# A gated mix of linear attention and an MLP block: wk by column halves, a second x chunk turned on PE, LN1 and w4 moved around the M stage

## The chip, the cores and the metric

The kernel runs on one core of one Trainium2 chip. The metric is the time of one execution on the device, in microseconds (us), as the median of several runs. The engines are TensorE (PE; its weight loads are shown as PEld), VectorE (DVE), ScalarE (ACT), GpSimd (POOL) and SyncE (SP). SP, ACT and POOL also issue DMA transfers.

## What is computed

One input x of 2048 rows and 640 columns goes through two blocks, whose results are mixed row by row with a gate:

```python
g = sigmoid((x * gate_w).sum(-1, keepdims=True))
qkv = x @ wqkv                                   # 32 heads of 20
pq, pk = phi(q), phi(k)                          # phi(t) = (t + 1 if t > 0 else exp(t)) + 1e-6
kv = einsum("bhsd,bhse->bhde", pk, v);  z = pk.sum(over s)
a = (pq @ kv) / (pq @ z + 1e-6)  @ wo            # linear attention
h = gelu(layernorm(x) @ w1)                      # B block
hs = (the four column groups of h, shifted by +1, -1, +2, -2 rows) @ w2
x1 = x + hs
b = x1 + gelu(layernorm(x1) @ w3) @ w4           # w3: 640 x 1728, w4: 1728 x 640
out = g * a + (1 - g) * b
```

Everything is bfloat16 in memory, with float32 sums.

## The kernel before

Rows are cut into 16 chunks (tiles) of 128, and into four tiles of 512 for the second half. Columns of 640 are five blocks of 128 (`DC`), or two halves of 320 (`HD`), the most that the code puts into one PSUM bank. All PSUM tiles are pairs of banks from one pool of four (`pair()`). The order of the instructions on every engine is the order in which the code writes them; the framework adds the waits. DMA queues are in order too: SP carries nearly all transfers.

The stages, in PE's order:

- **Start and K** (lines 126 to 225). x chunk 0 (line 126), gate_w and the five row blocks of wk, 128 x 640 each (`load_wk`, lines 128 to 132), are issued in turn on SP and ACT. Then SP issues seven DMA transposes (`load_xT`, line 133) that bring x chunks 1 to 15 in turned form into `xT`, then wq, x itself, wv, w1, wo, w2 and w3. Chunk 0 alone is turned on PE (lines 206 to 215): five transposes into two PSUM tiles (`turns`), each copied to `xT` by DVE; gate_w is turned in between and copied into column 640 of `wk_sb`, so that the K matmuls also give the gate's logit. `warmup` (line 200) issues filler matmuls on a constant: before the first work, and one of 256 columns between the row blocks of chunk 0. `k_mm` (line 186) does one chunk: for each of the five row blocks a left (320) and a right (321) matmul. `k_evac` copies the logit out and applies phi (`phi`, lines 177 to 184: one ACT and two DVE instructions).
- **Q** (`q_unit`, line 228), ten units of 1024 rows.
- **G** (`g_unit`, line 302): pk-transposed times x, with the statistics of the first layer norm (LN1) between the units, and `ln1_apply` (line 292), which normalises a chunk on DVE and turns it by a DMA transpose on SP into `lnxT[t]`. Three tiles of 512 rows are applied here.
- **w1 of tiles 0 and 1, kv, denominators** (`w1_unit`, line 336; `kv_unit`; `den_mm` and `den_evac`, lines 243 to 254, with a long DVE reciprocal). After w1 of tile 1 come LN1's last tile (lines 391 and 392), the release of the first stage's buffers, and the load of w4 on POOL's queue (lines 396 to 398).
- **M** (`m_unit`, line 373): kv times wo, five units of 16 small matmuls, each evacuated by ACT (line 381); then `r_unit`.
- **w2 of tile 0 with the second layer norm (LN2)** (`w2_unit`, line 408; `ln2_apply`, line 428, again with DMA transposes on SP), then w1 of tiles 2 and 3.
- **The loop over four tiles** (line 548): w3 with gelu (`w3_unit`), w2 of the next tile, attention's product with M (`att_unit`), then w4 (`w4_tile`) and the stores.

The kernel's own lines that the change touches:

Of the kernel before, what the change touches and what calls it, by code (L numbers as in the profile page):

```python
# [9 lines left out]
BF16 = mybir.dt.bfloat16  # L10
# [6 lines left out]
def kernel(  # L17
# [13 lines left out]
    nc = tc.nc  # L31
    P = 128
    S, D = A_x.shape[1], A_x.shape[2]
    F = B_w3.shape[1]
    H, Dh = 32, 20
    NCH = S // P
    TS = 512
    NT = S // TS
    CPT = TS // P
    DC = D // P  # L40
    HD = D // 2
    FF = F // P
    FR = F - FF * P
# [13 lines left out]
    wqkv_v = A_wqkv.rearrange("(c p) f -> p c f", p=P)  # L57
# [11 lines left out]
    def pair():  # L69
        return ps.tile([P, 2, 512], F32, name="pp")  # L70


    x_sb = const.tile([P, NCH, D + 2], BF16)
# [12 lines left out]
    ident = const.tile([P, P], BF16)  # L86
    g5 = const.tile([DC, P], BF16)
# [19 lines left out]
    wk_sb = st1.tile([P, DC, D + 16], BF16)  # L107
    gT = wk_sb
    xT = st1.tile([P, DC, S], BF16)
# [5 lines left out]
    sp, aq, gq = nc.sync, nc.scalar, nc.gpsimd  # L115

    def load_x(c0, c1):
        sp.dma_start(x_sb[:, c0:c1, 0:D], x2[c0 * P:c1 * P, :].rearrange("(c p) d -> p c d", p=P))

    def load_xT(c0, c1):  # L120
        sp.dma_start_transpose(xT[:, :, c0 * P:c1 * P], x2[c0 * P:c1 * P, :])

    def load_wk(q, dc):
        q.dma_start(wk_sb[:, dc, 0:D], A_wqkv[dc * P:(dc + 1) * P, D:2 * D])

    load_x(0, 1)
    aq.dma_start(g5[:], gate_w.rearrange("(c p) -> c p", p=P))
    load_wk(sp, 1)
    load_wk(aq, 0)
    load_wk(aq, 2)  # L130
    load_wk(sp, 3)
    load_wk(aq, 4)
    for c0, c1 in ((1, 2), (2, 3), (3, 4), (4, 6), (6, 8), (8, 12), (12, 16)):
        load_xT(c0, c1)
    sp.dma_start(wq_sb, wqkv_v[:, :, 0:D])
    load_x(1, 8)
    load_x(8, 12)
    load_x(12, 16)
    sp.dma_start(wv_sb[:], wqkv_v[:, :, 2 * D:3 * D])
# [37 lines left out]
    def phi(dst, src, n):  # L177
        e = e_p.tile([P, 1024], BF16, name="e")
        ev = e[:, 0:n]
        if len(src.shape) == 3:  # L180
            ev = ev.rearrange("p (h e) -> p h e", h=src.shape[1])
        nc.scalar.activation(ev, src, ACT.Exp)  # L182
        nc.vector.tensor_scalar(e[:, 0:n], e[:, 0:n], 1.0, 1e-6, op0=ALU.min, op1=ALU.add)  # L183
        nc.vector.scalar_tensor_tensor(dst, src, 0.0, ev, op0=ALU.max, op1=ALU.add)

    def k_mm(pt, c, dcs, hfs=(0, 1), last=DC - 1):
        for dc in dcs:
            for hf in hfs:
                n = HD + hf
                nc.tensor.matmul(pt[:, hf, 0:n], lhsT=xT[:, dc, c * P:(c + 1) * P],  # L190
                                 rhs=wk_sb[:, dc, hf * HD:hf * HD + n], start=(dc == 0), stop=(dc == last))

    def k_evac(pt, c):
        nc.scalar.copy(ylog[:, c:c + 1], pt[:, 1, HD:HD + 1])
        phi(pk[:, c, :].rearrange("p (h e) -> p h e", h=2), pt[:, :, 0:HD], D)
# [4 lines left out]
    def warmup(n, w=TS):  # L200
        for i in range(n):
            nc.tensor.matmul(warm[:, 1, 0:w], lhsT=one[:, 0:P], rhs=one[:, 0:w], start=True, stop=True)

    warmup(6)
    warmup(3, P)
    kp = pair()
    turns = [(pair()[:, 0, :].bitcast(BF16), a, b) for a, b in ((0, 2), (2, DC))]
    tg = warm[:, 0, :].bitcast(BF16)
    for n, (ptb, a, b) in enumerate(turns):
        for dc in range(a, b):  # L210
            nc.tensor.transpose(ptb[:, (dc - a) * P:(dc - a + 1) * P], x_sb[:, 0, dc * P:(dc + 1) * P], ident[:])
        nc.vector.tensor_copy(xT[:, a:b, 0:P], ptb[:, 0:(b - a) * P].rearrange("p (c s) -> p c s", c=b - a))
        if n == 0:
            nc.tensor.transpose(tg[:, 0:DC], g5[:], ident[0:DC, 0:DC])
            nc.vector.tensor_copy(wk_sb[:, :, D], tg[:, 0:DC])
    warmup(3, P)
    for dc in range(DC):
        k_mm(kp, 0, (dc,))
        if dc < DC - 1:
            warmup(1, 2 * P)  # L220
    k_evac(kp, 0)
    for c in range(1, NCH):
        pt = pair()
        k_mm(pt, c, range(DC))
        k_evac(pt, c)
# [17 lines left out]
    def den_mm():  # L243
        pt = pair()
        for j in range(DC):
            for t in range(NT):
                nc.tensor.matmul(pt[32 * t:32 * (t + 1), 0, :], lhsT=zbd[:, j, :], rhs=pqT[:, j, t * TS:(t + 1) * TS],  # L247
                                 start=(j == 0), stop=(j == DC - 1))
        return pt

    def den_evac(pt):
        nc.scalar.activation(pt[:, 1, :], pt[:, 0, :], ACT.Copy, bias=1e-6)
        with nc.allow_low_precision(reason="rounded after a float32 division, as a copy would"):
            nc.vector.reciprocal(r_bf[:], pt[:, 1, :])
# [9 lines left out]
    def scale_t(t):  # L264
        sl = pqT[:, :, t * TS:(t + 1) * TS]
        nc.vector.tensor_tensor(sl, sl, rb[:, t:t + 1, :].broadcast_to([P, DC, TS]), op=ALU.mult)
# [25 lines left out]
    def ln1_apply(c):  # L292
        t, cc = divmod(c, CPT)
        if cc == 0:
            lnxT[t] = lnx_p.tile([P, DC, TS], BF16, name="lnxT")
        lnx = work.tile([P, D], BF16, name="ln")
        nc.vector.tensor_scalar(lnx[:], x_sb[:, c, 0:D], mv1[:, c, 0:1], rstd1[:, c:c + 1],
                                op0=ALU.subtract, op1=ALU.mult)
        nc.sync.dma_start_transpose(lnxT[t][:, :, cc * P:(cc + 1) * P], lnx[:])
# [55 lines left out]
    def kv_unit():  # L355
        pt = pair()
        for g in range(NG):
            n = heads[g] * Dh
            for fc in range(DC):
                nc.tensor.matmul(pt[:, g // 3, (g % 3) * GW:(g % 3) * GW + n], lhsT=wv_sb[:, fc, row0[g]:row0[g] + P],  # L360
                                 rhs=gT[:, fc, 0:D].rearrange("p (j h i) -> p j h i", j=DC, h=H)
                                 [:, :, head0[g]:head0[g] + heads[g], :], start=(fc == 0), stop=(fc == DC - 1))
        for b, (q, g) in enumerate(pairs_qg):
            h0, h1 = max(8 * q, head0[g]), min(8 * q + 8, head0[g] + heads[g])
            a0, a1 = h0 - head0[g], h1 - head0[g]
            m = bmask5 if g == 5 else bmask
            base = (g % 3) * GW
            nc.vector.tensor_tensor(
                kvT[:, b, :, 4 * (h0 - 8 * q):4 * (h1 - 8 * q)],
                pt[:, g // 3, base:base + heads[g] * Dh].rearrange("p (j a) -> p j a", j=DC)[:, :, 4 * a0:4 * a1],  # L370
                m[:, 4 * a0:4 * a1].unsqueeze(1).broadcast_to([P, DC, 4 * (a1 - a0)]), op=ALU.mult)
# [14 lines left out]
        w1_unit(0, fcs)  # L386
    kv_unit()
    den_evac(den_mm())
    for fcs in w1_split:
        w1_unit(1, fcs)  # L390
    for cc in range(CPT):
        ln1_apply(3 * CPT + cc)
    s1.close()
    w4p = ctx.enter_context(tc.tile_pool(name="w4p", bufs=1))
    w4_sb = w4p.tile([P, FF + 1, D], BF16)
    nc.gpsimd.dma_start(w4_sb[:, 0:FF, :], B_w4[0:FF * P, :].rearrange("(c p) f -> p c f", p=P))
    nc.gpsimd.dma_start(w4_sb[0:FR, FF, :], B_w4[FF * P:F, :])
    nc.gpsimd.dma_start(w4_sb[FR:P, FF, :], B_w4[FF * P:F, :])
    h2p = ctx.enter_context(tc.tile_pool(name="h2p", bufs=1))
    x1p = ctx.enter_context(tc.tile_pool(name="x1p", bufs=8))  # L400
    st = {}
# [26 lines left out]
    def ln2_apply(t, cc):  # L428
        if cc == 0:
            st[t]["lnT"] = lnx_p.tile([P, DC, TS], BF16, name="lnxT")  # L430
        ln = work.tile([P, D], BF16, name="ln")
        nc.vector.tensor_scalar(ln[:], st[t]["x1"][cc][:], st[t]["mv"][:, cc, 0:1], st[t]["rstd"][:, cc:cc + 1],
                                op0=ALU.subtract, op1=ALU.mult)
        nc.sync.dma_start_transpose(st[t]["lnT"][:, :, cc * P:(cc + 1) * P], ln[:])
# [100 lines left out]
    for fcs in w1_split:  # L535
        w1_unit(2, fcs)
        if fcs[0] == 0:
            ln2_apply(0, CPT - 1)
    scale_t(0)
    scale_t(1)  # L540
    for fcs in w1_split:
# [48 lines left out]
```

## Time and profile before

| | us |
|---|---|
| median of 4 runs | 267.38 |
| lowest, highest | 267.05, 267.63 |
| the profiled execution | 267.53 |
| its span, first to last instruction | 265.0 |
| DVE busy | 139.6 |
| ACT busy | 84.2 |
| POOL busy | 22.8 |
| K stage, from PE's first matmul of it to its last | 5.59 to 27.99 |
| M stage, from its first matmul to the first of w2 | 85.2 to 88.5 |

The granted TensorE clock is full from 4.18 us on, and the mean over the span is 1.000. The DMA queues moved 23.62 MB; the share of busy time of the 16 DMA engines is highest in the first 45 us, where all weights and x come in, and it is near full there. After that only the layer norms' transposes, w4 and the stores are left.

A line of the chain of waits is: start, length, engine and what it did; the line number is that of the kernel. A line of the timeline adds the operation, the output and the inputs, the shape, and in brackets the idle time of the engine before it with what ended it.

### The profile page before, as it was taken

To read this page: it belongs to the slowest core of one execution; us is meant where nothing else is said; L and a number is where in the kernel's file an instruction comes from. 1 tells how busy PE (TensorE), PEld (TensorE's weight loads), DVE (VectorE), ACT (ScalarE), POOL (GpSimd) and SP (SyncE) were. 2 spreads that over 40 slices of the span, in tenths; PEclk is the share of its full clock that TensorE was granted. 3 is DMA by queue.
4 is the path that set the end of the run, shared out by engine and by line. 5 is a ranking of instruction groups with operands and counts; after the bars stand their busy time and mean duration, and the time that the engine had idled before them with its cause. 6 is when DMAs were issued, how large, how long until landed. Compare 5 with 4: busy or idle time off the path is not lost.

```text
span 265.0 us, 4251 instructions
## 1 busy us (share of the span) xinstructions
PE 259.1 (98%) x1728; PEld 162.1 (61%) x1744; DVE 139.6 (53%) x270; ACT 84.2 (32%) x122; POOL 22.8 (9%) x58
## 2 busy tenths in 40 slices
PE   7999999999999999999999999999999999999994
PEld 4777555788754654555567556567555566455663
DVE  1688778899946797955412364503464413122132
ACT  1455454321165735622420313330222340333100
POOL 7100010012223040001000001000001000000000
PEclk9999999999999999999999999999999999999999
DMA  7999978016668942000132000042000042000011
GB/s 173 199 194 370 375 238 326 0 28 123 124 116 249 200 87 52 0 0 2 25 74 77 25 0 2 9 90 77 25 0 2 1 99 76 25 0 2 0 49 49
DMA packets 44749, 23.62 MB, mean 89 GB/s; under 512 B 35450, under 2 KB 43642, under 8 KB 44730
## 3 DMA queue, kind: packets, MB, share of 16 engines
q1 hardware_dynamic: 43792, 20.57, 30.8%
q0 software_dynamic: 496, 2.29, 2.7%
q10 hardware_dynamic: 442, 0.49, 0.5%
q8 instruction: 13, 0.21, 0.4%
q14 instruction: 6, 0.05, 0.1%
HBM read 12.21 MB, written 2.62 MB: 56 GB/s over the span
## 4 chain that ended last, share of the span: by engine, by line
PE 95%; DMA 2%; ACT 1%; issue 0%; ACTq 0%; DVE 0%
PE pp L479 22%; PE pp L462 21%; PE pp L307 8%; PE pp L190 8%; PE pp L415 8%; PE pp L446 8%; PE pp L341 8%; PE pp L232 8%; DMA wk_sb<-in_A_wqkv_dram 2%; PE pp L467 1%; PE pp L488 1%; ACT m_sb L381 1%; PE pp L360 1%; PE pp L247 0%; PE pp L379 0%
## 5 line engine op out<-in xcount | busy, mean ns | idle before, releaser
L470 ACT ACTIVATE h<-pp 128x1024 bf16<-128x1024 f32 (+1 forms) x28 | 27.8, 992 | 102.8 <-PE pp L462 94.4
L462 PE MATMUL pp<-lnxT,w_sb 128*128 128x512 bf16 x249 | 59.8, 379 | 0.6
L479 PE MATMUL pp<-w_sb,h 128*128 128x320 bf16 x416 | 57.9, 299 | 0.0
L479 PEld LDWEIGHTS <-h 128*128 128x128 bf16 x416 | 40.0, 98 | 17.0 <-issue 1.9
L462 PEld LDWEIGHTS <-w_sb 128*128 128x128 bf16 x260 | 25.4, 98 | 26.7
L495 DVE SCALAR_TENSOR_TENSOR oc<-pp,omg,x 128x640 bf16<-128x640 f32 x15 | 12.9, 881 | 44.0 <-PE pp L488 27.1
L449 DVE SCALAR_TENSOR_TENSOR x<-pp,gate,x 128x640 f32<-128x640 f32 x16 | 13.9, 868 | 29.4 <-PE pp L446 29.4
L182 ACT ACTIVATE e<-pp 128x640 bf16<-128x640 f32 (+1 forms) x26 | 21.5, 826 | 9.6 <-PE pp L232 9.6
L446 PE MATMUL pp<-m_sb,pqT 128*128 128x320 bf16 x160 | 24.3, 299 | 0.0
L418 DVE TENSOR_TENSOR x<-pp,x_sb 128x640 f32<-128x640 f32 x16 | 13.1, 819 | 21.0 <-PE pp L415 21.0
L415 PE MATMUL pp<-w_sb,hsT 128*128 128x320 bf16 x160 | 23.9, 299 | 0.1
L190 PE MATMUL pp<-wk_sb,xT 128*128 128x320 bf16 (+1 forms) x160 | 22.4, 299 | 0.7 <-DMA wk_sb<-in_A_wqkv_dram 0.7
L307 PE MATMUL pp<-x_sb,pk 128*128 128x320 bf16 (+1 forms) x160 | 22.3, 300 | 0.0
L232 PE MATMUL pp<-xT,hsT 128*128 128x512 bf16 x98 | 21.6, 379 | 0.1
L307 PEld LDWEIGHTS <-pk 128*128 128x128 bf16 x160 | 18.8, 117 | 3.5
L415 PEld LDWEIGHTS <-hsT 128*128 128x128 bf16 x160 | 15.7, 98 | 8.2 <-issue 0.2
L446 PEld LDWEIGHTS <-pqT 128*128 128x128 bf16 x160 | 15.7, 98 | 7.7
L190 PEld LDWEIGHTS <-xT 128*128 128x128 bf16 x160 | 15.6, 98 | 6.8 <-issue 0.8
L341 PE MATMUL pp<-lnxT,w_sb 128*128 128x512 bf16 x77 | 17.8, 379 | 0.2
L232 PEld LDWEIGHTS <-hsT 128*128 128x128 bf16 x100 | 11.8, 118 | 9.7
L277 POOL TENSOR_SCALAR rstd<-mv 128x4 f32<-128x4 f32 (+1 forms) x11 | 3.4, 313 | 148.3 <-DVE mv L283 148.3
L183 DVE TENSOR_SCALAR e<-e 128x640 bf16<-128x640 bf16 (+1 forms) x26 | 9.6, 369 | 8.8 <-ACT e L182 7.3
(79 smaller groups left out, 195.8 us busy)
## 6 DMA issues: line engine op xcount, KB each, us to landing
out_dram<-oc SPq DMA_DIRECT2D x15, 160.0 KB, 1.8
w_sb<-in_B_w_dram SPq DMA_DIRECT2D x1, 2160.0 KB, 8.7
w_sb<-in_B_w_dram POOLq DMA_DIRECT2D x1, 2080.0 KB, 11.1
x_sb<-in_A_x_dram SPq DMA_DIRECT2D x2, 640.0 KB, 10.4
x_sb<-in_A_x_dram SPq DMA_DIRECT2D x1, 1120.0 KB, 8.0
wo_sb<-in_A_wo_dram SPq DMA_DIRECT2D x6, 160.0 KB, 8.3
hsT<-in_A_wqkv_dram SPq DMA_DIRECT2D x1, 800.0 KB, 5.5
m_sb<-in_A_wqkv_dram SPq DMA_DIRECT2D x1, 800.0 KB, 11.2
```

The lines of the kernel that those rows point to most:

```text
L182: nc.scalar.activation(ev, src, ACT.Exp)
L190: nc.tensor.matmul(pt[:, hf, 0:n], lhsT=xT[:, dc, c * P:(c + 1) * P], rhs=wk_sb[:, dc, hf * HD:hf * HD + n], start=(dc == 0), stop=(dc == ...
L232: nc.tensor.matmul(pt[:, t % 2, :], lhsT=wq_sb[:, dc, :].rearrange("p (m j) -> p j m", j=DC)[:, j], rhs=xT[:, dc, t * TS:(t + 1) * TS], st ...
L307: nc.tensor.matmul(pt[:, hf, 0:HD + hf], lhsT=w, rhs=x_sb[:, c, hf * HD:(hf + 1) * HD + hf], start=(c == 0), stop=(c == NCH - 1))
L341: nc.tensor.matmul(pt[:, i, :], lhsT=w, rhs=lnxT[t][:, dc, :], start=(dc == 0), stop=(dc == DC - 1))
L415: nc.tensor.matmul(pt[:, hf, 0:HD], lhsT=hsT[:, fc, 2 + c * P:2 + (c + 1) * P], rhs=w2_sb[:, fc, hf * HD:(hf + 1) * HD], start=(fc == 0), ...
L418: nc.vector.tensor_tensor(x1[:].rearrange("p (h e) -> p h e", h=2), pt[:, :, 0:HD], x_sb[:, c, 0:D].rearrange("p (h e) -> p h e", h=2), op ...
L446: nc.tensor.matmul(pt[:, hf, 0:HD], lhsT=pqT[:, j, c * P:(c + 1) * P], rhs=m_sb[:, j, hf * HD:(hf + 1) * HD], start=(j == 0), stop=(j == D ...
L449: nc.vector.scalar_tensor_tensor(x1, pt[:, :, 0:HD], gate[:, c:c + 1], x1, op0=ALU.mult, op1=ALU.add)
L462: nc.tensor.matmul(pt[:, k, :], lhsT=w3_sb[:, dc, fc * P:(fc + 1) * P], rhs=lnT[:, dc, :], start=(dc == 0), stop=(dc == DC - 1))
L470: nc.scalar.activation(h2[:, 2 * i * TS:2 * i * TS + n], pt[:].rearrange("p h e -> p (h e)")[:, 0:n], ACT.Gelu_apprx_tanh)
L479: nc.tensor.matmul(dst, lhsT=st[t]["h2"][:, fc * TS + cc * P:fc * TS + (cc + 1) * P], rhs=w4_sb[:, fc, a:b], start=start and fc == 0, stop ...
```

## The change

Three edits, in the order of the code.

The loads: wk comes in five transfers by column halves (left halves of blocks 0-1, 2-3 and 4; right halves of blocks 0-2 and 3-4), ACT's first transfer is a wk block and not gate_w, and x chunk 1 is loaded plain as SP's third transfer, in place of its DMA transpose.

The start of K: chunks 0 and 1 are both turned on PE by `x_turn`, into the two banks of one PSUM pair. Chunk 0's left matmuls 0 to 3, the turn of chunk 1, then the left matmul 4 of chunk 0 and the left ones of chunk 1 are done first, the right ones of both after them. The fillers between the blocks go; five of 128 columns stand behind the first turn, one before chunk 1's first matmuls.

Around M: LN1's last tile is applied before w1 of tile 1 and not after it; w4 is loaded on SP's queue, behind LN2's transposes of tile 0 and w1 of tile 2, and not on POOL's ahead of M.

```diff
-    def load_wk(q, dc):
-        q.dma_start(wk_sb[:, dc, 0:D], A_wqkv[dc * P:(dc + 1) * P, D:2 * D])
+    def load_wk(q, d0, d1, hf):
+        q.dma_start(wk_sb[:, d0:d1, hf * HD:(hf + 1) * HD],
+                    wqkv_v[:, d0:d1, D + hf * HD:D + (hf + 1) * HD])
 
     load_x(0, 1)
+    load_wk(aq, 0, 2, 0)
+    load_wk(sp, 2, 4, 0)
+    load_wk(aq, 4, 5, 0)
+    load_x(1, 2)
     aq.dma_start(g5[:], gate_w.rearrange("(c p) -> c p", p=P))
-    load_wk(sp, 1)
-    load_wk(aq, 0)
-    load_wk(aq, 2)
-    load_wk(sp, 3)
-    load_wk(aq, 4)
-    for c0, c1 in ((1, 2), (2, 3), (3, 4), (4, 6), (6, 8), (8, 12), (12, 16)):
+    load_wk(aq, 0, 3, 1)
+    load_wk(sp, 3, 5, 1)
+    for c0, c1 in ((2, 3), (3, 4), (4, 6), (6, 8), (8, 12), (12, 16)):
         load_xT(c0, c1)
     sp.dma_start(wq_sb, wqkv_v[:, :, 0:D])
-    load_x(1, 8)
+    load_x(2, 8)
...
     warmup(6)
-    warmup(3, P)
-    kp = pair()
-    turns = [(pair()[:, 0, :].bitcast(BF16), a, b) for a, b in ((0, 2), (2, DC))]
+    kp = [pair(), pair()]
+    turns = pair()
     tg = warm[:, 0, :].bitcast(BF16)
-    for n, (ptb, a, b) in enumerate(turns):
-        for dc in range(a, b):
-            nc.tensor.transpose(ptb[:, (dc - a) * P:(dc - a + 1) * P], x_sb[:, 0, dc * P:(dc + 1) * P], ident[:])
-        nc.vector.tensor_copy(xT[:, a:b, 0:P], ptb[:, 0:(b - a) * P].rearrange("p (c s) -> p c s", c=b - a))
-        if n == 0:
-            nc.tensor.transpose(tg[:, 0:DC], g5[:], ident[0:DC, 0:DC])
-            nc.vector.tensor_copy(wk_sb[:, :, D], tg[:, 0:DC])
-    warmup(3, P)
-    for dc in range(DC):
-        k_mm(kp, 0, (dc,))
-        if dc < DC - 1:
-            warmup(1, 2 * P)
-    k_evac(kp, 0)
-    for c in range(1, NCH):
+
+    def x_turn(c):
+        ptb = turns[:, c, :].bitcast(BF16)
+        for dc in range(DC):
+            nc.tensor.transpose(ptb[:, dc * P:(dc + 1) * P], x_sb[:, c, dc * P:(dc + 1) * P], ident[:])
+        nc.vector.tensor_copy(xT[:, 0:2, c * P:(c + 1) * P], ptb[:, 0:2 * P].rearrange("p (c s) -> p c s", c=2))
+        nc.vector.tensor_copy(xT[:, 2:DC, c * P:(c + 1) * P], ptb[:, 2 * P:D].rearrange("p (c s) -> p c s", c=DC - 2))
+
+    x_turn(0)
+    warmup(5, P)
+    k_mm(kp[0], 0, (0, 1, 2, 3), (0,))
+    x_turn(1)
+    k_mm(kp[0], 0, (4,), (0,))
+    warmup(1, P)
+    k_mm(kp[1], 1, (0, 1), (0,))
+    nc.tensor.transpose(tg[:, 0:DC], g5[:], ident[0:DC, 0:DC])
+    nc.vector.tensor_copy(wk_sb[:, :, D], tg[:, 0:DC])
+    k_mm(kp[1], 1, (2, 3, 4), (0,))
+    for c in range(2):
+        k_mm(kp[c], c, range(DC), (1,))
+        k_evac(kp[c], c)
+    for c in range(2, NCH):
         pt = pair()
...
     den_evac(den_mm())
+    for cc in range(CPT):
+        ln1_apply(3 * CPT + cc)
     for fcs in w1_split:
         w1_unit(1, fcs)
-    for cc in range(CPT):
-        ln1_apply(3 * CPT + cc)
     s1.close()
     w4p = ctx.enter_context(tc.tile_pool(name="w4p", bufs=1))
     w4_sb = w4p.tile([P, FF + 1, D], BF16)
-    nc.gpsimd.dma_start(w4_sb[:, 0:FF, :], B_w4[0:FF * P, :].rearrange("(c p) f -> p c f", p=P))
-    nc.gpsimd.dma_start(w4_sb[0:FR, FF, :], B_w4[FF * P:F, :])
-    nc.gpsimd.dma_start(w4_sb[FR:P, FF, :], B_w4[FF * P:F, :])
...
         w1_unit(2, fcs)
         if fcs[0] == 0:
             ln2_apply(0, CPT - 1)
+    nc.sync.dma_start(w4_sb[:, 0:FF, :], B_w4[0:FF * P, :].rearrange("(c p) f -> p c f", p=P))
+    nc.sync.dma_start(w4_sb[0:FR, FF, :], B_w4[FF * P:F, :])
+    nc.sync.dma_start(w4_sb[FR:P, FF, :], B_w4[FF * P:F, :])
     scale_t(0)
```

More of the change, by code (lines that the diff above doesn't have):

```diff
@@ L184, in phi, with k_mm @@
         nc.vector.scalar_tensor_tensor(dst, src, 0.0, ev, op0=ALU.max, op1=ALU.add)
-    def k_mm(pt, c, dcs, hfs=(0, 1), last=DC - 1):
+    def k_mm(pt, c, dcs, hfs=(0, 1)):
         for dc in dcs:
@@ L190, in k_mm @@
                 nc.tensor.matmul(pt[:, hf, 0:n], lhsT=xT[:, dc, c * P:(c + 1) * P],
-                                 rhs=wk_sb[:, dc, hf * HD:hf * HD + n], start=(dc == 0), stop=(dc == last))
+                                 rhs=wk_sb[:, dc, hf * HD:hf * HD + n], start=(dc == 0), stop=(dc == DC - 1))
     def k_evac(pt, c):
```

## The prediction

> **What bounds the kernel now.** I read the page first, then the chain of waits of the first 10 us, the timeline of the same stretch, the busy table by windows, and last the chain around the M stage.
>
> ```profile
> span 265.0 us, 4251 instructions
> ...
> PE 259.1 (98%) x1728; PEld 162.1 (61%) x1744; DVE 139.6 (53%) x270; ACT 84.2 (32%) x122; POOL 22.8 (9%) x58
> ...
> PE   7999999999999999999999999999999999999994
> ```
>
> TensorE has work in 98% of the span; only the first and the last slice are below 9. A stage that is moved off DVE, SP or POOL is worth nothing unless PE waited for it. So I look for places where PE idles or runs filler. The start is one:
>
> ```profile
> 1.39 4.16 DMA wk_sb<-in_A_wqkv_dram
> 5.55 0.04 issue
> 5.59 0.43 PE pp L190 x2
> 6.02 0.11 PE pp L202
> ...
> 7.17 0.11 PE pp L202
> 7.28 2.73 PE pp L190 x20
> ```
>
> Columns are start, length, what. The first real matmul waits for a block of wk that landed at 5.55. Four fillers (L202) of 0.11 then stand between the pairs of row tile 0, which keeps them in step with the rest of wk. After that the K stage runs at 2.73/20 = 0.136 us a matmul, so 1.36 a row tile; tile 1 starts at 7.39 and tile 2 at 8.75.
>
> ```profile
> 4.12 0.29 DVE L212 COPY xT<-pp 128x256 bf16<-128x256 bf16 x1 [4.12 <-PE pp L211]
> 4.13 0.35 PE L211 MATMUL pp<-ident,x_sb 128*128 128x128 bf16 x3
> ...
> 4.52 0.36 DVE L212 COPY xT<-pp 128x384 bf16<-128x384 bf16 x1
> ...
> 5.59 0.43 PE L190 MATMUL pp<-wk_sb,xT 128*128 128x320 bf16 x2 [0.70 <-DMA wk_sb<-in_A_wqkv_dram]
> ```
>
> Here are the prices of a turned x chunk: five transposes, then two copies by DVE of 0.29 and 0.36. x was ready in its turned form at 4.88, and PE still sat 0.70 us on wk. So the start is bound by the DMA, and the table of windows (time, busy time of PE, PEld, DVE, ACT, POOL, then PE clock, DMA share and GB/s) says that the DMA engines were not full between 2.5 and 3.5:
>
> ```profile
> 2.50:3.00 0.50, 0.50 (x3) 0.22 (x2) 0.00 (x0) 0.26 (x1) 0.40 (x2) 1.00 0.92 154
> 3.00:3.50 0.50, 0.50 (x4) 0.22 (x3) 0.00 (x0) 0.50 (x1) 0.42 (x2) 1.00 0.68 215
> 4.50:5.00 0.50, 0.33 (x3) 0.21 (x3) 0.36 (x2) 0.00 (x0) 0.43 (x2) 1.00 1.07 384
> ```
>
> The second place is the M stage:
>
> ```profile
> 85.23 0.69 PE pp L379 x16
> 85.91 0.02 issue
> 85.94 2.49 ACT m_sb L381 x4
> 88.42 0.04 issue
> 88.47 5.59 PE pp L415 x40
> ```
>
> What ends last there is ACT's evacuation of M (2.49), not DVE, SP or the w4 load.
>
> **What the Trainium skill says.** "DMA: Bandwidth & Descriptors", section "Issuing engines are not separate DMA queues": transfers issued from different engines share the same 16 DMA engines and interleave. The trace agrees: counting 16 landing events to a transfer, x chunk 0 landed at 3.12, then by turns SP's wk 1 at 5.33, ACT's wk 0 at 5.55, SP's wk 3 at 5.78, ACT's wk 2 at 6.21, ACT's wk 4 at 6.70. "TensorE: Matmul & The Clock Gate", "Part 4: PE-mode transpose": the result goes to PSUM, so a DVE copy must follow; the trace has 0.31 us for one transpose before the clock rose at 4.18 and 0.22 after, 0.107 and 0.055 apart. "PSUM — Partial Sum Buffer", "PSUM bank collisions raise a hardware error": two engines must not be in one bank at once. The new x_turn puts all five transposes into one bank, so I let the first copy wait for the fifth; no row of before shows that wait, since there the two parts lie in two tiles. Same page as Part 4, "Part 1: The HAM clock gate": the clock falls back after about 3.4 us without work; PE's 0.70 us of idle did not lower it here.
>
> **The change part by part.** Call L01, L23, L4 the left halves of wk (column blocks of rows 0-1, 2-3, 4), R02 and R34 the right ones, x1 the second x chunk, T the time at which x1 has landed and the left matmuls 0 to 3 are through.
>
> Removed: four fillers of 0.107 = 0.43; the wait of the third transpose for gate_w (4.13 - 3.88 = 0.25, hidden anyway by the 0.70); one DMA transpose, xT chunk 1. Added on PE: five transposes (5 x 0.055 = 0.27, the clock being up), one filler 0.055.
>
> From T on: transposes start at T+0.05, the last at T+0.27, ends T+0.49; first copy T+0.53 to T+0.82; second copy to T+1.17. PE meanwhile has matmul dc 4 of chunk 0 and the filler (0.19, to T+0.52), then waits until T+0.86. Two left matmuls to T+1.13, the gate_w transpose to T+1.19, after the second copy three more to T+1.62. The gate_w copy (0.17 in before) is through by about T+1.56, so it is hidden, by 0.06. Then ten right matmuls: tile 2 starts at T+2.98. In before it starts at 8.75. **The break-even is T = 5.77.** A saving before that point is a saving of the whole: the row tiles follow at 1.36 each.
>
> T is the cost that the trace doesn't show. The floor: the six long fillers end at 3.35, five cold transposes 0.107 apart, last at 3.82+0.31, copies at 4.17 to 4.46 and to 4.80, so matmuls 0 to 3 are over at 5.11. By places in the queue: x1 is SP's third transfer of 160 KB, as wk 3 was: 5.78 (15 of its 16 DMA engines by 5.42). L23 is SP's second, as wk 1 was: 5.33 (15 of 16 by 4.58), and its two matmuls (0.04 + 0.27) end at 5.64. For earlier: ACT's first wk is issued at 0.79 and not at 1.39, into the half empty windows above. For later: ACT's data now compete from the start, and 640-byte rows: the last output stores have such rows at a median of 32 ns a packet against 55 for 1280 bytes, so 16% more per byte (0.17 us on the 400 KB of left halves at 16 x 1280 bytes / 55 ns = 372 GB/s). I take T = 5.6; ends 5.11 and 6.3 (5.78 + 0.17 + 80 KB more in front, 0.22, and a slow DMA engine's 0.1). That is a gain of 0.17, at best 0.66, at worst a loss of 0.53.
>
> Right halves: needed from T+1.62 = 7.2. In before 960 KB had landed by 6.70; 160 KB more at 372 GB/s are 0.44, and the first blocks come first. Hidden, with little to spare. DMA transposes: SP reaches chunk 2's after four plain issues of about 0.42, at 2.6; chunk 2 (landed 7.88 in before, needed 8.75) has room. The tightest is chunks 8 to 11: landed 16.58, used at 16.92. One transpose less (0.78 between chunks 2 and 3) against 0.44 for the plain chunk moves it some 0.3 earlier; with the 0.34 of room a gain up to 0.6 passes.
>
> K evacuation: tiles 0 and 1 come 0.68 apart, not 1.36; DVE needs 1.27 a tile and falls behind, but the buffer of tile 2 is free at about T+7.3 and wanted at T+8.4. No stall.
>
> LN1 of tile 3 ahead of w1_unit(1): four DVE rows, 1.52 in all (87.12 in before), now behind the reciprocal that ends at 83.80, so to 85.3, before the hx copies at 85.89. SP issues its four transposes from 84.2, behind LN1 tile 2's, which ended at 80.34. Neither was on the chain: 0. Without that cover the hx copies would come late by what is over, and with them the first matmul of L415 that reads tile 1's rows, over 2 us later. w4: POOL loses 2.5 us of issue at 79.17, and nothing of POOL's is due before 92.11: 0. On SP it stands behind the LN2 transposes (last issue ends 101.73); nothing of SP's follows until 130.25, and w4 is first read at 130.4; before it took 11.1 us to land, so by 113. The last LN2 transpose landed at 103.15, w3's first weights load at 104.47: 1.3 us of room. 0, bounds 0 and +0.3.
>
> Sum: 267.53 (the profiled execution, 265.0 of span and 2.5 around it) - 0.17 = 267.36. The median of the four runs is 0.15 below that execution, so 267.2 to 267.4; I say 267.3.
>
> **The rivals.** (a) No change, T 5.25 to 6.3: 267.3. For it: both places in the queue give 5.6 to 5.8, beside the break-even. Against: both ends are open. Chance 0.40. (b) Faster: T near the floor, because ACT's early issue fills the idle DMA windows and no DMA engine lags as the one that made wk 1 land 0.75 after its other 15. T = 5.15 gives 0.62, 266.9; on the median 266.8. Against: in before each early transfer had such a lagging engine. Chance 0.33. (c) Slower: the halves double the rows (896 in front of and with x1, 512 with wk 3). If the 128-row transfers' spacing (about 0.45 from landing to landing) is a price per row, 3.5 ns, not per byte, x1 lands 384 x 3.5 = 1.35 later, T = 6.95, 268.7; it decides from T = 6.3 on, and PE would be seen waiting at the second chunk's transposes. Against: 256-byte packets take 18 ns and 640-byte stores 32, so packets are paid by size. Chance 0.27 with the tail of (a). (d) The change doesn't do what it says for M: its wait is ACT's, so the second half is worth 0; this is part of all three.
>
> **How the numbers follow.** A measurement of this kernel can tell about 0.2% (0.53 us) from no change. Faster 0.33, within 0.40, slower 0.27. The likeliest case's own range is 266.85 to 267.9. The range goes to (b)'s time with a little below it, 266.6, and half way to (c), 268.2.
>
> **What would show it.** First L190 matmul at about 4.9 to 5.3; x1's landing near 5.6; tile 2's first matmul near 8.6; PE idle of about 0.35 behind the second transposes; the M stage still 3.3 us with ACT m_sb in its chain; no PE wait at w3's or w4's first matmul. It is wrong if tile 2 starts before 8.2 or after 9.3, or if chunk 8 waits for its DMA transpose, or if the M stage changes its length.

## The result, and the profile after

| | before | after |
|---|---|---|
| median, us (runs) | 266.88 (64) | 267.69 (43) |
| lowest, highest | 266.27, 268.64 | 267.02, 268.80 |
| ratio of after to before, with its 95% interval | | 1.0030 [1.0022, 1.0039] |
| the profiled execution | 267.53 | 268.42 |
| its span | 265.04 | 265.58 |
| what lies around the span | 2.49 | 2.84 |

The changed kernel is slower by 0.8 us, 0.3%. The time lies in the predicted range, but by luck: the prediction started from four runs of before with a median of 267.38, and over 64 runs it is 266.88, so its starting point was 0.5 too high, and a loss of 0.8 took the place of the gain of 0.17 that was worked out. The direction was not the one held likeliest, and the cases of the prediction did not have the main causes. The page of the kernel after, its counts and the row of PE in 40 slices:

```profile
span 265.6 us, 4248 instructions
...
PE 259.8 (98%) x1729; PEld 161.9 (61%) x1745; DVE 139.5 (53%) x272; ACT 84.0 (32%) x122; POOL 20.4 (8%) x55
...
PE   8999999999999999999999999999999999999994
```

PE is as full as before. Two counts matter later: PEld has 1745 where it had 1744 (five transposes more and four fillers less; each brings one weight load and one matmul; matmul records can be missing, so the weight loads are the count to trust), and POOL has 55 where it had 58 (its three w4 issues). The chain of waits of the first 10 us of the kernel after:

```profile
3.55 0.53 PE pp L214 x5
4.08 0.53 PE pp L204 x5
4.62 1.10 PE pp L192 x4
5.71 0.35 PE pp L214 x5
6.07 0.02 issue
6.09 0.30 DVE xT L215
6.39 0.05 issue
6.44 0.45 PE pp L192 x2
6.88 0.11 PE pp L225
6.99 5.01 PE pp L192 x36
```

L214 is the turn, L204 the fillers, L192 the K matmuls, L225 the turn of gate_w. The four left matmuls take 1.10, 0.27 each, because in this execution the clock rose only at 5.72. The copy of the second chunk (L215) is the last wait of this stretch. The timeline of the same stretch shows the two waits, for x1 on PEld and for the turned chunk on PE (idle time and releaser in brackets); a third line, from 16 us on, shows one more at tile 8:

```profile
5.51 0.37 PEld L214 LDWEIGHTS <-x_sb 128*128 128x128 bf16 x5 [0.39 <-DMA x_sb<-in_A_x_dram]
...
6.44 0.45 PE L192 MATMUL pp<-wk_sb,xT 128*128 128x320 bf16 x2 [0.19 <-DVE xT L215]
...
17.02 0.39 PEld L192 LDWEIGHTS <-xT 128*128 128x128 bf16 x4 [0.31 <-DMA xT<-in_A_x_dram]
```

By landing events x1 was there at 5.47, against T = 5.6 in the prediction. Tile 2 starts at 8.71, against 8.75 before: a gain of 0.04 in place of 0.17. At tile 8 it is lost again: chunk 8's DMA transpose landed at 16.98, so tile 8 starts at 17.03, 8.32 after tile 2, where before it came 8.17 after (16.92). The prediction had named a wait there as a sign of being wrong. The busy table by windows (columns as before) shows why the data came early: the stretch that had been half empty is filled, 305 and 347 GB/s where there had been 154 and 215.

```profile
2.50:3.00 0.50, 0.50 (x3) 0.14 (x1) 0.00 (x0) 0.15 (x1) 0.39 (x2) 1.00 0.98 305
3.00:3.50 0.50, 0.50 (x4) 0.14 (x3) 0.00 (x0) 0.50 (x1) 0.42 (x2) 1.00 1.12 347
```

Around M, the chain:

```profile
85.34 0.69 PE pp L388 x16
86.03 0.02 issue
86.05 2.49 ACT m_sb L390 x4
88.54 0.04 issue
88.58 3.42 PE pp L421 x24
```

M still takes 3.24 us, with the same 2.49 of ACT in it. So between these two executions nothing is lost up to here but 0.11 (w2 at 88.58 for 88.47), which is there from tile 8 on. PE's and DVE's last work keeps it (DVE ends at 262.33 for 262.21). The rest of the 0.54 of span lies behind the last work, in the closing steps of POOL (0.48 between two of them, for 0.17; the drain itself then takes 0.17, for 0.04), and 0.35 more lies outside the span. These are records of the trace that none of the shown views has (times in us). q8 and q14 are two queues that carry instructions. They are taken for PE's and POOL's: q8 moves 0.21 MB, and PE has 3474 of the 4248 instructions; q14's fetches change with POOL's number of instructions, as the experiments show.

```
                     POOL: semaphores cleared   then its drain at   instruction fetches after the last work
before                   264.60                     264.77           q8 16 KB 266.83 to 267.85
after                    264.69                     265.17           q14 8 KB 266.21 to 266.51, q8 16 KB 267.36 to 268.73
```

### The profile page after: what moved, and what is told of

Read it like the earlier page. It is cut to its first block, busy times and chain, and to the rows that moved or that the text cites. A ratio compares the mean times of both kernels' runs of the same rounds, so it can differ in the third digit from the quotient of the medians.

```text
span 265.6 us, 4248 instructions
## 1 busy us (share of the span) xinstructions
PE 259.8 (98%) x1729; PEld 161.9 (61%) x1745; DVE 139.5 (53%) x272; ACT 84.0 (32%) x122; POOL 20.4 (8%) x55
## 4 chain that ended last, share of the span: by engine, by line
PE 97%; ACT 1%; issue 0%; DVE 0%
PE pp L485 22%; PE pp L468 21%; PE pp L192 9%; PE pp L316 8%; PE pp L421 8%; PE pp L452 8%; PE pp L350 8%; PE pp L241 8%; PE pp L204 1%; PE pp L473 1%; PE pp L494 1%; ACT m_sb L390 1%; PE pp L369 1%; PE pp L256 0%; PE pp L214 0%
## 5 line engine op out<-in xcount | busy, mean ns | idle before, releaser
L192 PE MATMUL pp<-wk_sb,xT 128*128 128x320 bf16 (+1 forms) x160 | 23.2, 304 | 0.2 <-DVE xT L215 0.2
L192 PEld LDWEIGHTS <-xT 128*128 128x128 bf16 x160 | 15.4, 98 | 6.9 <-DVE xT L215 0.4
L186 DVE SCALAR_TENSOR_TENSOR pk<-pp,e 128x640 bf16<-128x640 f32 x16 | 13.2, 825 | 1.7
```

## The experiments

Single runs of the kernel before went from 266.0 to 268.6, so two profiled executions can't settle a difference of 0.8. Beside the ratio of the medians two means over all runs are therefore used: the span, and the time outside the span. For before on the chip of the first comparison only times are on record, so the mean span of the whole change can be set only against before on other chips. On the chips of the experiments before had medians of 266.63 to 266.70, spans of 264.90 to 264.94 and 1.81 to 1.87 outside. Standard errors of an experiment's mean span are 0.03 to 0.11 where none is given, in brackets where larger.

| kernel | ratio and interval | mean span | outside | PEld count |
|---|---|---|---|---|
| the whole change | 1.0030 [1.0022, 1.0039] | 265.63 | 2.21 | 1745 |
| start_only | 1.0022 [1.0010, 1.0033] | 265.24 | 2.14 | 1745 |
| mid_only | 1.0013 [1.0004, 1.0021] | 265.24 | 1.80 | 1744 |
| w4_only | 1.0011 [1.0000, 1.0022] | 265.31 | 1.82 | 1744 |
| w4_pool_late | 1.0115 [1.0086, 1.0143] | 268.20 (0.39) | 1.67 | 1744 |
| w4_pool_fill | 1.0008 [0.9998, 1.0017] | 265.10 | 1.79 | 1744 |
| w4_mixed | 1.0008 [0.9997, 1.0019] | 264.91 | 1.89 | 1744 |
| before_fill1 | 1.0014 [1.0003, 1.0024] | 264.96 | 2.14 | 1745 |
| start_fill4 | 1.0016 [1.0006, 1.0026] | 265.29 | 1.87 | 1744 |
| before_split | 1.0003 [0.9987, 1.0019] | 264.81 | 2.21 | 1744 and one wait |
| before_split_less | 0.9984 [0.9976, 0.9992] | 264.62 | 1.74 | 1742 and one wait |
| before_less | 0.9992 [0.9980, 1.0004] | 264.81 | 1.73 | 1742 |
| start_xt_early | 1.0035 [1.0019, 1.0051] | 265.65 (0.15) | 2.07 | 1745 |
| start_xt_split4 | 1.0043 [1.0031, 1.0054] | 265.58 | 2.20 | 1744 and one wait |
| start_one_right | 1.0034 [1.0014, 1.0053] | 265.71 (0.24) | 1.77 | 1744 |
| after_trim | 1.0015 [1.0004, 1.0027] | 265.18 | 1.87 | 1744 |

**The two halves of the change: start_only and mid_only.** The first is the kernel before with the new loads and the new start of K alone; the second has the old start, LN1's move and w4 on SP's queue.

```diff
-    for cc in range(CPT):              # mid_only: behind w1_unit(1)
-        ln1_apply(3 * CPT + cc)
+    for cc in range(CPT):              # ahead of it
+        ln1_apply(3 * CPT + cc)
...
-    nc.gpsimd.dma_start(w4_sb[:, 0:FF, :], ...)   # ahead of M
+    nc.sync.dma_start(w4_sb[:, 0:FF, :], ...)     # behind ln2_apply(0, CPT - 1)
```

> The changed loads and start of K alone; LN1 and w4 as before. Theory S (the loss is in the K stage: SP's first DMA transpose waits for a landing, issued at 3.80 where 2.6 was expected, chunk 8's transpose lands after PE wants it): the whole loss is here, 0.5 to 0.9 us over before, and PE waits for xT at chunk 8. Theory E (the loss is at the end of the program: with no transfer left on POOL's queue, POOL's last steps took 0.39 us longer in the profile): at most +0.15 us, POOL's last steps short again.

> LN1's last tile ahead of w1 of tile 1 and w4 on SP behind LN2, start as before. Theory S: no change, within 0.1 us. Theory E: 0.4 to 0.8 us slower, the chain up to the last product as before, the time after the last store longer.

Both are slower, and in different places. start_only adds 0.30 to the mean span and 0.30 outside it; mid_only adds 0.30 to the span and nothing outside. The chain of waits of start_only, whose clock rose at 4.11, shows the new start without cold matmuls:

```profile
4.47 0.72 PE pp L192 x4
5.19 0.01 issue
5.20 0.47 PE pp L214 x5
5.67 0.02 issue
5.69 0.30 DVE xT L215
5.99 0.05 issue
6.04 0.45 PE pp L192 x2
6.49 0.11 PE pp L225
6.59 10.06 PE pp L192 x73
16.65 0.02 issue
16.67 1.40 PE pp L192 x9
```

x1 landed at 5.16 here, so the copy starts at T+0.53 and the matmuls at T+0.88, as predicted (0.53, 0.86). The timeline has the starts of what follows:

```profile
6.04 0.45 PE L192 MATMUL pp<-wk_sb,xT 128*128 128x320 bf16 x2 [0.20 <-DVE xT L215]
6.42 0.17 PE L225 MATMUL pp<-ident,g 5*128 5x5 bf16 x1
6.53 0.72 PE L192 MATMUL pp<-wk_sb,xT 128*128 128x320 bf16 x4
```

From the first of the two left matmuls to the next left one 0.49 pass, where the prediction had 0.33. The turn of gate_w is what was priced too low: it starts 0.11 later than the pair's 0.27 would have it and takes 0.11, so 0.22 in place of 0.06. (The 0.45 of the pair is not its price: it counts to the end of the second one. In before the pair has 0.43, from 5.59, and its filler starts at 5.86 all the same.) Tile 2 starts at 8.31, T + 3.15 and not T + 2.98. At tile 8 PE waited for chunk 8 here too: it landed at 16.62, and tile 8 comes 8.36 after tile 2.

**Where the second half loses: w4_only and w4_pool_late.** The one moves w4 to SP behind LN2 and leaves LN1; the other issues w4 at the same new place, but from POOL.

```diff
-    nc.gpsimd.dma_start(w4_sb...)    # ahead of M, three transfers
+    nc.sync.dma_start(w4_sb...)      # w4_only: behind LN2 of tile 0
+    nc.gpsimd.dma_start(w4_sb...)    # w4_pool_late: the same place, POOL's queue
```

> Only w4 moved to SP behind LN2. Theory S: no change. Theory E: as slow as the one with LN1 moved too, 0.4 to 0.8 us.

> w4 issued at the same late place, but still on POOL's queue: place against queue. Theory S: no change. Theory E: no change, since POOL keeps its transfers; if it is slower by 0.4 us or more, the place is what counts and not the queue.

w4_only has all of mid_only's loss (265.31 for 265.24, the errors together 0.12), so LN1's move is worth 0 as far as these runs tell. No PE wait stands at w3 or w4 in it. What is longer is POOL's end: from the clearing of the semaphores to the drain 0.47, for 0.17 before. w4_pool_late was meant to keep POOL's instructions and showed something else, a loss of 3.3 us. Its chain of waits at the first w3 matmuls (L459):

```profile
100.25 6.62 DMA lnxT<-ln
106.87 0.14 issue
107.00 3.95 PE pp L459 x10
```

LN2's last transpose, issued on SP, takes 6.62 us to land while w4's 2.2 MB run beside it from another queue. w4_only differs in that queue alone and has no such wait. In the kernel after w4 stands behind it on the same queue, and the transpose, issued at 100.64, landed at 103.26. PE idles 2.44 us, and the table of windows of the same kernel shows the second price (PEclk is the third number from the end):

```profile
107.00:111.00 4.00, 4.00 (x12) 1.53 (x13) 2.38 (x2) 1.12 (x3) 0.00 (x0) 0.57 0.70 236
```

The clock was at half from 107.53 to 110.94. So the queue that the change chose is the right one for that place; the prediction's 0 at LN2 holds for SP alone.

**What it is on POOL: w4_pool_fill and w4_mixed.** The first is w4_only with eight small memsets on POOL where w4's issue was. The second moves w4's two larger transfers to SP and leaves the last, 80 KB, on POOL at its old place.

```diff
+    pad = const.tile([P, CPT], F32)
-    nc.gpsimd.dma_start(w4_sb...)    # three, ahead of M
+    for _ in range(8):               # w4_pool_fill; w4_mixed: one of the three stays
+        nc.gpsimd.memset(pad[:], 0.0)
```

> w4 on SP behind LN2 (nothing of w4 on POOL), and eight small memsets on POOL where its three transfers stood. Theory P (the end is longer because POOL reaches its last steps with fewer instructions behind it, so that a block of instructions is fetched there): POOL's step after the semaphore clear is short again, about 0.17 us from clear to drain instead of 0.47, and no 8 KB instruction fetch after the end; +0.3 us goes back to 0. Theory D (it is the transfers themselves on POOL): still 0.47, and still 0.3 us slower than before.

> The two larger transfers of w4 on SP behind LN2, the last one (80 KB) still on POOL ahead of M. Theory D: the end is short again, 0.17 us from clear to drain, time as before within 0.1 us. Theory P: between the two, or still long, since POOL has some five instructions less than before.

In both POOL's end is short again (0.13 and 0.17), though w4 comes over SP late. Without w4, POOL has eight instructions less (three issues and five that wait for or signal semaphores); the memsets give eight back. w4_mixed has lost only two of them, so by itself it doesn't tell the transfers from the count; w4_pool_fill, which has no transfer of w4 on POOL, does. The row of POOL's instruction queue in the pages' third part (queue, packets, MB, share) tells what changed. Of the kernel after:

```profile
q14 instruction: 5, 0.04, 0.0%
```

Of w4_pool_fill:

```profile
q14 instruction: 6, 0.05, 0.1%
```

With fewer instructions on POOL one of the six instruction fetches on q14 is missing inside the span (before, it came at 83.2) and comes after it. All three kernels with five (after, mid_only, w4_only) have a long end, 0.46 to 0.48; of the others none has. The mean span of w4_mixed is that of before (264.91), that of w4_pool_fill lies between (265.10). So POOL's longer end goes with the number of its instructions and not with the transfers. What it is worth is less sure: mid_only and w4_only are 0.30 and 0.37 over before, w4_mixed gives all of it back, and w4_pool_fill only about half.

**What lies outside the span: before_fill1, start_fill4, before_less.** The changed start has one weight load and one matmul more than the old one. before_fill1 is the kernel before with one filler more, start_fill4 is start_only with one less, before_less is before with two less.

```diff
-    warmup(3, P)
+    warmup(4, P)     # before_fill1; before_less: warmup(1, P)
...
-    warmup(5, P)     # start_only
+    warmup(4, P)     # start_fill4
```

> The kernel before with one filler of 128 columns more ahead of the first K matmul, where PE waits for wk anyway: two rows more on PE, as the changed start has. Theory F (the changed start's time outside the span, 0.26 us longer at the median, comes from PE's last instruction fetch, which two more PE rows pull into the timed stretch): span unchanged within 0.1 us, time less span 0.2 to 0.3 us longer at the median. Theory L (it comes from the changed loads or the span): no change at all.

> The changed start alone, with four fillers behind the first turn instead of five: PE's rows as many as before. Theory F: time less span back to about 1.73 at the median, total 0.25 us better than with five, so about 0.25 us over before. Theory L: as with five, 0.5 us over before.

> The kernel before with two fillers less, without the cut: four PE rows less. Theory F: time less span 1.7 to 1.75 at the mean (1.82 before), span unchanged within 0.1. With the cut and the same four rows less the span was 264.62 and 0.28 below before: if the cut is what did that (chunk 8's landing), the span here is back at 264.9; if the fillers did it, it is 264.6 here too.

One filler of 0.055 us, put in where PE waits anyway, leaves the span alone (264.96 for 264.90) and adds 0.33 outside it. Taking it from the new start gives 0.27 back (2.14 to 1.87) and changes nothing in its span. The count of weight loads in the page's first part, of before_fill1:

```profile
PE 260.1 (98%) x1745; PEld 162.0 (61%) x1745; DVE 139.5 (53%) x270; ACT 84.2 (32%) x122; POOL 22.8 (9%) x58
```

and of before_less:

```profile
PE 260.1 (98%) x1742; PEld 161.8 (61%) x1742; DVE 139.5 (53%) x270; ACT 84.2 (32%) x122; POOL 22.9 (9%) x58
```

The fetches on q8 are blocks of 16 KB, the last of them inside the span at about 242. One more follows the last work in some executions, and the measured time then ends 0.31 to 0.32 us before that fetch's end: in the profiles of before (267.53, fetch to 267.85), start_only (266.54, 266.85), w4_only (268.05, 268.36), after (268.42, 268.73) and before_split (267.82, 268.13). Executions with more than 2.2 us outside the span are 9 to 14 in 100 of before, 41 of before_fill1, 43 of the whole change and none of before_split_less. So PE's number of instructions shifts how often the time is long. That it does so by where it stands against a block's end is likely and not shown: before and w4_only have the late fetch too, with 1744, and the profile of start_fill4 has 2.00 outside without one in its trace.

**The turned chunks at tile 8: before_split, before_split_less, start_xt_early, start_xt_split4, start_one_right.** Where chunks 8 to 11 are one DMA transpose they land at 16.3 to 17.2 (start_one_right apart), which is where tile 8 is due: it comes 8.17 after tile 2. The chain of waits of w4_only, which has the old start, runs over SP's issues:

```profile
9.52 7.09 DMA xT<-in_A_x_dram
16.62 0.05 issue
16.66 1.40 PE pp L190 x9
```

Tile 8 starts 0.04 to 0.05 after the landing, so with these landings of the old start (16.31 to 16.75) one that reaches tile 2 before 8.2 to 8.6 is cut off here; in the kernel after (16.98), before 8.9. These kernels cut that transfer in two, issue the first turned chunk ahead of gate_w, or make one transfer of the right halves; start_xt_split4 is start_xt_early with the cut and one filler less.

```diff
-    ((1, 2), (2, 3), (3, 4), (4, 6), (6, 8), (8, 12), (12, 16))
+    ((1, 2), (2, 3), (3, 4), (4, 6), (6, 8), (8, 10), (10, 12), (12, 16))   # before_split
-    warmup(3, P)
+    warmup(1, P)                                                            # before_split_less: both
...
-    aq.dma_start(g5[:], ...)          # start_xt_early: gate_w behind load_xT(2, 3)
-    load_wk(aq, 0, 3, 1)
-    load_wk(sp, 3, 5, 1)
+    load_wk(aq, 0, 5, 1)              # start_one_right, with 4 fillers
```

> The kernel before with the DMA transpose of chunks 8 to 11 cut in two (8-9, 10-11). Theory C (in most executions chunk 8's landing at about 16.6, and not the start, sets the end of the K stage, so that an earlier start is lost again): chunk 8's half lands near 14.6, tile 8 follows tile 2 at the pace of 8.17 us, and the span is 0.2 to 0.3 us shorter at the mean. Theory N (chunk 8's wait is no bound, only the first start counts): span unchanged within 0.1.

> The kernel before with the cut, and two fillers of 128 columns less ahead of the first K matmul: four PE rows less. Theory F: time less span at its floor, 1.65 to 1.75 in nearly all executions, and with the cut the fastest of all, 0.3 us under before.

> The changed start alone with gate_w's transfer issued behind the first DMA transpose, so that one transfer less stands ahead of it and SP need not wait for a landing (3.57 to 3.80 in three profiles). First transpose issued near 2.7, chunk 8 landing earlier. If that wait is what costs the changed start its time: span 0.2 us or more below the 265.24 of the start alone. If the DMA engines set the landing: chunk 8 lands at about 16.6 all the same and the span stays within 0.1.

> The same with chunks 8 to 11 cut in two and four fillers instead of five: the changed start with its three side costs taken away. If they were its whole loss, it equals or beats the kernel before (span 264.9 or less); against the kernel before with the cut alone it is still behind by the 0.2 us by which tile 2 starts later.

> The changed start alone with four fillers, and the right halves of wk in one transfer on ACT instead of two: seven transfers stand ahead of the first DMA transpose, not eight. If the eighth is what makes SP wait (3.57 to 3.80), the first transpose is issued near 2.2 and chunk 8 lands 0.3 us or more earlier. If that wait costs the changed start its time, the span falls 0.2 us or more below the 265.29 of the start with four fillers; if the late second x chunk costs it, the span stays within 0.1 of that, or rises because the right halves land later.

before_split brings chunk 8 in at 14.37, and its mean span is 264.81 for 264.90, less than the 0.2 to 0.3 that was expected; and the cut adds one semaphore instruction to PE, which goes with 0.4 more outside, much as a filler does. Without two fillers (before_split_less) both come together: 266.22 us, the fastest of all, 0.9984 of before. Of its 0.4 the fillers alone (before_less) give about 0.2, with an interval that holds no change too; the rest would be the cut's, but 264.62 and 264.81 with errors of 0.07 don't settle its size.

start_xt_early did not do what it was meant to: in the changed kernels SP issues its first turned chunk at 3.57 to 3.80 and not at 2.6, and it still did (3.76), since SP waits for the landing of an earlier transfer whose semaphore is used again: it is ACT's first wk block, which landed at 3.74 here and at 3.78 in the kernel after, where the issue is at 3.80. gate_w's transfer, though moved, was issued at 2.29 and had the last of the eight semaphores that these transfers use in turn. gate_w came late instead, at 6.87, and PE waited for it. So this run and start_xt_split4 say nothing of the early transpose; the latter shows that chunk 8 at 13.80 alone does not pay for a tile 2 at 9.03. start_one_right, with one transfer less, takes SP's wait away (first issue at 2.23, chunk 8 at 14.46), and is no faster. Its chain of waits:

```profile
2.42 5.38 DMA wk_sb<-in_A_wqkv_dram
7.80 0.05 issue
7.85 4.27 PE pp L191 x30
```

The right halves land at 7.80 here, for 6.69 in the kernel after, and tile 2 starts at 9.22. The turned chunks run beside them now, so SP's wait may have protected them; the run doesn't tell this from the one larger transfer in place of two.

**The sum: after_trim.** The whole change with four fillers for five and eight memsets on POOL, so without the two losses that have nothing to do with what the change moves.

```diff
-    warmup(5, P)
+    warmup(4, P)
...
+    for _ in range(8):
+        nc.gpsimd.memset(pad[:], 0.0)
```

> The whole change, with four fillers instead of five and eight small memsets on POOL in the place of the w4 transfers: the two side costs taken away, everything else of the change kept. If the account is additive: about 0.7 us below the whole change (267.69), so 267.0 to 267.1, 0.3 to 0.4 us over before, the rest being the start. If the rest is still 0.8 us over before, the two side costs are not the cause.

266.99 us: 0.7 under the median of the whole change. Outside the span it has what before has (1.87), and 0.28 more in the span, as start_only (0.30) and start_fill4 (0.39) have. But w4_pool_fill, with the same memsets and the old start, kept 0.20, which should come on top; with errors of 0.07 to 0.1 the sum is right in the main and not to 0.1 or 0.2.

## Why the prediction was wrong, point by point

The loss has three parts of about the same size, and the single measurements add up to it: the start 0.30 in the span (start_only), POOL's end 0.30 in the span (mid_only), PE's one instruction pair more 0.30 outside (start_only), 0.9 against 0.8 measured. These parts have errors of about 0.1 each.

- **The break-even T = 5.77 failed; T did not.** "In before it starts at 8.75" was read from one execution, in which wk's block 0 landed at 5.55; in the others with the old start it landed between 4.28 and 5.01. The table shows what a start costs from profile to profile (before_less and before_split_less, with two fillers less, and the three starts with other loads are left out):

| start | clock rise, tile 2, tile 8 of each profile | means of tile 2 and tile 8 |
|---|---|---|
| old | 3.60, 8.11, 16.80; 3.82, 8.05, 16.35; 4.18, 8.75, 16.92 (before); 4.95, 8.22, 16.66; 5.13, 8.21, 16.62; 5.71, 8.51, 16.69; 6.53, 8.83, 17.00; 6.63, 8.90, 17.08 | 8.45, 16.77 |
| new | 4.11, 8.31, 16.67; 5.72, 8.71, 17.03 (after); 6.21, 9.20, 17.37; 6.82, 8.98, 17.16 | 8.80, 17.06 |

  x1 landed at 5.16, 5.47, 5.97 and 5.34 in the new ones, 5.49 on the mean: 0.11 better than the 5.6 that was taken. From there tile 2 took 3.31 on the mean, not 2.98: 0.33 worse. About half of that is the turn of gate_w (0.16 in start_only, which took 3.15); the rest comes in the three whose clock rose later. And the reference was 8.45, not 8.75: 0.30 worse. The predicted -0.17 with these three is +0.35, the difference of the means. The mean of the old clock rises is 0.65 earlier, so some of the 0.33 is chance; at equal rise (5.71 and 5.72; 3.82 and 4.11) the new start is 0.20 to 0.26 later.
- **"A gain up to 0.6 passes at chunk 8" failed.** The new start's chunk 8 landed at 16.98, and was expected some 0.3 before 16.58. SP issued its first transpose at 3.80 and not at 2.6; that wait was not in the working. Even T at its floor would have been cut off at tile 8, so rival (b) could not have won all of its 0.6.
- **w4's 0 failed, in a place that was not looked at.** At LN2 and w3 it is 0 as worked out: the last transpose landed at 103.26 and w3's first weights were loaded at 104.59. The cost came at the program's end, and goes with the fewer instructions on POOL and the fetch that then comes there. The bound of +0.3 had the size but not the place.
- **PE's instructions were costed by their time alone.** The new start has one weight load and one matmul more, which stand before a wait and so were worth nothing; they were worth 0.3 outside the span. No case of the prediction had this.
- **Rival (c), the price of rows, is refuted.** x1 landed 5.2 to 6.0, not at 6.95, and the 640-byte packets of the halves took 32 ns at the median, as the stores did, not the 55 of the longer ones. The kernel is slower, but not by that mechanism.
- **Right:** LN1's move 0 (w4_only has all of mid_only's loss); M unchanged with ACT's 2.49 in its chain; the right halves hidden (6.69, first used at 7.3); no stall by K's evacuation; the idle DMA windows filled by ACT's early wk. That the queues of several engines share the DMA engines (the Trainium skill, "DMA: Bandwidth & Descriptors", "Issuing engines are not separate DMA queues") is seen best in w4_pool_late, with its 6.62 us for one transpose.
- **The clock at the start was taken as fixed at 4.18**; it rises at 3.6 to 6.8 us, in both kernels. The page that the prediction cites, "TensorE: Matmul & The Clock Gate", says in "Part 1: The HAM clock gate" that the window of about 3.4 us is free-running. The runs agree: the rises spread over 3.2 us, the half clock of w4_pool_late lasted 3.41, and the stretches at full clock in all profiles last 102.40, 157.01, 259.41 or 262.83, which are 30, 46, 76 and 77 times 3.413. The prediction's "about 3.4 us without work" was too long as a rule for what is safe: in w4_pool_late the clock fell with 2.44 us without matmuls in the 3.41 before.

What stays open: how a missing fetch lengthens POOL's last steps (only the counts and the two times were seen); why w4_pool_fill keeps 0.2 of span with a short end, where w4_mixed keeps none; why the turn of gate_w takes 0.22; what decides from one execution to the next whether the time outside the span is long; and how the start's 0.3 divides among the late second chunk, gate_w's turn, the wait at tile 8 and matmuls at half clock.

## What to carry to other kernels

For a change that is worth tenths of a microsecond, take the reference of a break-even from several executions, not from one: here tile 2's start moved by 0.85 us between profiles with the same start. Split each measurement into the span and what lies around it, and count the instructions of each engine: here the times that changed outside the span, or only behind the last work, went with the number of instructions and not with the schedule. When a transfer is moved beside others that something waits for, try it behind them on the same queue: here that cost nothing at that place, and another queue cost 3.3.

## What the runs showed of the hardware that was not expected

- One filler more on PE lengthens the measured time by 0.3 us without moving the span, two less shorten it by 0.1: outside 1.73 (two fillers less), 1.81 to 1.87 (as before), 2.14 (one more), in a program of some 1745 weight loads.
- POOL's last step took 0.13 to 0.17 us with six instruction fetches of q14 inside the span, and 0.46 to 0.48 with five.
- PE is busy from about 0.83 on in all profiles, and the clock rises anywhere from 3.6 to 6.8 us; with it the first K matmuls take 0.14 or 0.27 us each, and tile 2 of the old start moves from 8.05 (rise at 3.82) to 8.90 (6.63). Rises and falls of the clock lie a whole number of times 3.413 us apart (30, 46, 76 or 77 in these profiles, 1 for the half clock).
- SP's plain transfers and turned chunks are in one queue, but a turned chunk can be held by a semaphore of a transfer of another queue: issue at 3.57 to 3.80 where eight transfers had taken a semaphore before it, at 2.23 where only seven had.
